# Casts of v moved from ScalarE to POOL in the first block, first normalises brought forward, feed-forward pieces let past waiting hashes

## The chip, the cores and the metric

The kernel runs on one core of one Trainium2 chip. A core has five engines that run side by side, each with its own list of instructions in a fixed order: TensorE (PE in the profile; its weight loads are PEld), VectorE (DVE), ScalarE (ACT), GpSimd (POOL) and SyncE (SP, which here only issues transfers). Sixteen DMA engines move data between the chip's memory and the core. The time is device time in microseconds of the whole program, and less is better.

## The reference

Two steps follow one another. The first is attention with hashed buckets: for each of 4 batches and 8 heads, 768 tokens of 64 features. Six sign bits of a random projection give each query and each key a bucket, and a query attends only to keys of its own bucket.

```
q_bits = (einsum('bhsd,dk->bhsk', q, proj) > 0);  k_bits likewise
q_bucket = sum(q_bits * 2**arange(6));            k_bucket likewise
scores = q @ k.T / 8, -1e9 where the buckets differ
x = softmax(scores) @ v
```

The second is a gated feed-forward layer over the 3072 rows of 512 features that the heads make together:

```
out = x + sigmoid(x @ w_res) * ((gelu(x @ w_gate) * (x @ w_val)) @ w_out)      # 512 -> 1536 -> 512
```

## The kernel before

**Tiling.** The work is cut into eight blocks: 4 batches times two halves of 384 query tokens (`c`). A block has four pairs of heads, and each pair six steps (two heads, three double key tiles), so 24 steps (`LB`). A step `i` is a score product (L579: 128 keys x 384 queries, twice), an exp on ScalarE (L583) and, two steps later in the list, the product with v (`attend`, L607), which TensorE sums into the one av bank in PSUM. After a pair's sixth step VectorE takes the reciprocal of the row sums (L620) and multiplies (L621), which gives `xtok` and frees the av bank for the next pair.

**The hash in the scores.** For each pair, `aug` holds 64 rows of q or k as bf16 and 7 rows made of the hash bits; one product over these 71 rows gives the score and a large penalty where the buckets differ. For the first batch `prep_tokens` fills it: TensorE transposes the tokens (L499), ScalarE and VectorE evacuate them to `trT` (L400), TensorE multiplies by the projection (L462), VectorE makes the bits from PSUM (L426), casts the 64 rows (L418, L416) and moves the bit rows (L436). Part of the second half's rows is cast later. From the second batch on `prep_blocks` does it otherwise: a 32x32 transpose on VectorE (L531), projection (L539), bits (L546), transfers from POOL's queue (L549) and casts (L554).

**v.** `cast_v` (L377) casts a pair's v to bf16 into `vaug`, with a column of ones. Pair 0 and all pairs from the second batch on are cast on POOL, pairs 1 to 3 on ScalarE.

**Feed-forward.** Once a block's four `xtok` are there they are transposed (on TensorE for block 0, L643 and L649; by DMA for later blocks, L629), the gate products run (L661, gelu on ScalarE, L665), and the rest (value L677 and L680, residual L689, output L701, L710, L713, L720) is dealt out in pieces between the attention steps of the next block. Gelu and exp need different tables on ScalarE, so the gelus stand together.

**Loads.** SP loads q, k and v; POOL loads the weights (L361), in the order `wg`, `wv`, `wr`, `wo`, in software-generated transfers that also cast to bf16. The loads of the second batch stand on SP behind a one-element transfer that waits for `wr` (L283).

**What sets the order.** The code first records operations with their engine, an assumed cost, what they read and write, and ring buffers of fixed depth (two score banks, one av bank, three general mm banks, three buffers each for the loaded q, k and v, and so on). `arrange` then plays them out on assumed clocks: on each engine it takes the earliest recorded operation that is ready and whose buffers are free, and emits the instructions in the order of the times it found. A buffer is given only in the order of recording (L186). On the chip each engine runs its list in that order, with semaphore waits. Where TensorE would be idle early on, small products on an idle or unused part of a bank (L830, L833) fill in; their results are not used.

Of the kernel before, what the change touches and what calls it, by code (L numbers as in the profile page):

```python
# [20 lines left out]
def kernel(  # L21
# [54 lines left out]
    made = {name: 0 for name in RINGS}  # L76

    class Buf:


        def __init__(self, ring, make):
            self.ring, self.make, self.tile, self.users, self.taken = ring, make, None, 0, False
            self.place = made[ring]
            made[ring] += 1

# [5 lines left out]
    class Op:  # L91
        __slots__ = ("eng", "cost", "emit", "bufs", "seq", "deps", "left", "users", "ready", "start",
                     "end", "land", "table", "size", "after", "lag", "margin", "opens", "closes", "held", "flight")

    def op(eng, cost, emit, r=(), w=(), table=None, size=0, after=(), lag=0.0, margin=0.0, opens=None, closes=None, held=False, flight=None):
# [8 lines left out]
        o.flight = flight  # L104
        o.seq, o.deps, o.users, o.ready, o.start = len(ops), set(), [], 0.0, None
        o.bufs = []
        for key in (*r, *w):
            b = key[0] if isinstance(key, tuple) else key
            if isinstance(b, Buf) and b not in o.bufs:
                o.bufs.append(b)  # L110
                b.users += 1
        for key in r:
# [23 lines left out]
    def arrange(warm_until, keep_warm):  # L136
# [9 lines left out]
        HOLDS = dict(DVE=("pair", "block"), SP=("xfer",), POOL=("xfer",), ACT=("gelu",))  # L146
        closed = set()
# [6 lines left out]
        def push(o):  # L154
            for e in o.cost:
                heapq.heappush(queue[e], (o.ready, o.seq))
# [6 lines left out]
        while seen < len(ops):  # L163
# [3 lines left out]
            for e in engines:  # L167
                while queue[e] and queue[e][0][0] <= t:
                    heapq.heappush(able[e], heapq.heappop(queue[e])[1])
# [3 lines left out]
                while able[e]:  # L173
                    s = heapq.heappop(able[e])
# [5 lines left out]
                    for b in o.bufs:  # L180
                        line = taken[b.ring]
                        if not b.taken:

                            at = more[b.ring] = more.get(b.ring, len(line) - 1) + 1
                            old = at - RINGS[b.ring]
                            if b.place != at or old >= 0 and gone.get(line[old], 1e9) > t:  # L186
                                fits = False
                    if o.table == "exp" and gelus:
                        fits = False
# [6 lines left out]
                    if fits and e != "PE":  # L196

                        for ready, other in queue[e]:
                            if other < s and ready < t + 0.5 * o.cost[e]:
# [4 lines left out]
                    skipped.append(s)  # L204
                for s in skipped:
                    heapq.heappush(able[e], s)
# [31 lines left out]
                for b in o.bufs:  # L238
# [3 lines left out]
                    b.users -= 1  # L242
                    if b.users == 0:
# [38 lines left out]
    def wait_weights():  # L282
        op("SP", 0.4, lambda: nc.sync.dma_start(mark, wr[0:1, 0, 0:1]), r=["wr"],  # L283
# [72 lines left out]
    mark = const.tile([1, 2], BF16, name="mark")  # L356
# [17 lines left out]
    mark = const.tile([1, 1], BF16, name="mark")  # L374


    def cast_v(n):  # L377
        b, j = pairs[n]
        s = staged[("v", n)]
        cost = VCAST if 0 < n < NPAIR else {"POOL": 0.85}  # L380

# [3 lines left out]
        op(None, cost, emit, r=[(s, 0)], w=[("vaug", b % 2, j)])  # L385

    VCAST = {"ACT": 0.85}
# [485 lines left out]
```

## Time and profile before

| | |
|---|---|
| median of 6 runs | 348.9 us (348.12 to 349.85) |
| the profiled execution's own time | 349.01 us |
| its span | 347.2 us |
| granted TensorE clock | 1.0 |
| exps of L583 | 192, 811 ns each, 149.8 us |
| casts of v | 13 on POOL, 3 on ScalarE (847 ns in the middle) |
| first gate product (L661) | 38.17 us |

The span runs from the first to the last instruction in the profile; the profiled execution took 1.8 us more. Times in the views are microseconds from the span's start. Busy times of matmuls are modelled ends of a pipeline, and the fillers count as busy, so a busy TensorE early in the span need not be a useful one. An engine's idle time is given with what ended it; what a stage costs is read from the stage, not from the average.

### The profile page before, as it was taken

The numbers are of one execution on the slowest core, as the hardware profiler recorded it, in microseconds if no ns is written. First come the engines' busy times: TensorE is split into PE (matmuls) and PEld (weight loads), VectorE is DVE, ScalarE is ACT, GpSimd is POOL, SyncE is SP. The second block draws the span as 40 slices with busy tenths as digits, with TensorE's granted clock in tenths as the row PEclk, the third lists the DMA queues.
The fourth block names the chain that finished last, engine by engine and source line by source line (L and its number), as shares of the span: only waits on it lengthen the run. The fifth ranks groups of instructions, "written<-read, shape, count | busy, mean of one in ns | idle before, by whom it ended". The sixth has DMA issues, their size and how long they took to land.

```text
span 347.2 us, 7664 instructions
## 1 busy us (share of the span) xinstructions
PE 337.0 (97%) x3052; PEld 200.9 (58%) x3076; DVE 190.4 (55%) x344; ACT 236.2 (68%) x341; POOL 61.6 (18%) x101
## 2 busy tenths in 40 slices
PE   8988999999999999999999999999999999999996
PEld 4645666555665566555665556655666556655654
DVE  4997137969689538896363425725052414523353
ACT  3989887755867668665777758675787858775410
POOL 0631000521336310314001220203000100001000
PEclk9999999999999999999999999999999999999999
DMA  7999999999997399987200120021000120012002
GB/s 237 348 215 208 195 159 153 134 174 167 158 149 101 85 192 165 148 92 115 67 13 18 51 71 0 18 55 47 32 14 12 44 72 2 17 49 74 0 2 91
DMA packets 116357, 34.23 MB, mean 99 GB/s; under 512 B 107802, under 2 KB 113698, under 8 KB 116322
## 3 DMA queue, kind: packets, MB, share of 16 engines
q1 hardware_dynamic: 109522, 22.27, 43.8%
q0 software_dynamic: 6496, 11.27, 13.7%
q8 instruction: 24, 0.39, 0.5%
q10 hardware_dynamic: 304, 0.20, 0.2%
q14 instruction: 11, 0.09, 0.1%
HBM read 29.36 MB, written 6.29 MB: 103 GB/s over the span
## 4 chain that ended last, share of the span: by engine, by line
PE 86%; DVE 8%; DMA 3%; ACT 2%; issue 1%; DVEq 0%
PE mm L677 18%; PE mm L661 17%; PE mm L701 16%; PE sc L579 15%; PE av L607 9%; PE mm L689 5%; PE mm L539 3%; DMA xT<-xtok 3%; DVE bits L426 2%; DVE aug L436 2%; ACT e L583 1%; PE idle L830 1%; DVE aug L418 1%; DVE xtok L621 1%; DVE trT L400 1%
## 5 line engine op out<-in xcount | busy, mean ns | idle before, releaser
L583 ACT ACTIVATE e<-sc 128x768 bf16<-128x768 f32 x192 | 149.8, 811 | 50.5 <-PE sc L579 50.1
L680 DVE TENSOR_TENSOR gh<-mm,gh 128x384 bf16<-128x384 f32 x96 | 53.4, 556 | 76.4 <-PE mm L677 62.2
L579 PE MATMUL sc<-aug 71*128 71x384 bf16 x384 | 92.4, 325 | 1.8 <-ACT e L583 1.7
L677 PE MATMUL mm<-xT,wv 128*128 128x384 bf16 x384 | 73.5, 326 | 0.0
L607 PEld LDWEIGHTS <-e 128*128 128x128 bf16 x1152 | 57.0, 97 | 24.0 <-issue 2.5
L701 PE MATMUL mm<-wo,gh 128*128 128x512 bf16 (+2 forms) x303 | 69.0, 362 | 0.4
L661 PE MATMUL mm<-xT,wg 128*128 128x384 bf16 x384 | 66.3, 326 | 1.1 <-DMA xT<-xtok 0.8
L665 ACT ACTIVATE gh<-mm 128x384 bf16<-128x384 f32 x96 | 45.6, 492 | 31.6 <-PE mm L661 31.3
L607 PE MATMUL av<-vaug,e 128*128 128x65 bf16 x1152 | 62.2, 193 | 1.4 <-DVE xtok L621 1.4
L661 PEld LDWEIGHTS <-wg 128*128 128x128 bf16 x384 | 37.0, 98 | 26.2 <-issue 1.8
L579 PEld LDWEIGHTS <-aug 71*128 71x128 bf16 x384 | 34.8, 98 | 29.2 <-issue 5.4
L677 PEld LDWEIGHTS <-wv 128*128 128x128 bf16 x384 | 34.0, 98 | 21.5 <-issue 3.1
L701 PEld LDWEIGHTS <-gh 128*128 128x128 bf16 x312 | 27.2, 98 | 26.0 <-issue 1.9
L710 DVE SCALAR_TENSOR_TENSOR y<-th,mm 128x512 f32<-128x512 bf16 x23 | 15.8, 687 | 45.7 <-PE mm L701 40.6
L549 POOL DMA_DIRECT2D aug<-bits x48 | 27.9, 585 | 68.7 <-DVE bits L546 68.3
L720 POOL DMA_DIRECT2D out_dram<-o x21 | 13.0, 620 | 134.0 <-DVE rec L620 106.3
L692 ACT ACTIVATE th<-mm 128x512 bf16<-128x512 f32 x24 | 14.4, 598 | 16.5 <-PE mm L689 16.5
L554 DVE TENSOR_SCALAR aug<-trT 64x1536 bf16<-64x1536 f32 x24 | 23.5, 979 | 1.1 <-PE sc L579 0.4
L689 PE MATMUL mm<-wr,xT 128*128 128x512 bf16 x81 | 22.9, 379 | 0.8
L384 POOL CAST vaug<-vs 128x768 bf16<-128x768 f32 x13 | 11.4, 874 | 46.8 <-DMA vs<-in_v_dram 32.5
L546 DVE TENSOR_SCALAR bits<-mm,shift 128x384 bf16<-128x384 f32 x24 | 13.6, 609 | 10.7 <-PE mm L539 10.5
L621 DVE TENSOR_TENSOR xtok<-av,rec 128x384 bf16<-128x384 f32 x32 | 17.8, 558 | 1.1
(58 smaller groups left out, 168.5 us busy)
## 6 DMA issues: line engine op xcount, KB each, us to landing
vs<-in_v_dram SPq DMA_DIRECT2D x16, 384.0 KB
out_dram<-o POOLq DMA_DIRECT2D x21, 256.0 KB, 2.5
qs<-in_q_dram SPq DMA_DIRECT2D x48, 96.0 KB
ks<-in_k_dram SPq DMA_DIRECT2D x48, 96.0 KB
wg<-in_moe_w_gate_dram POOLq DMA_DIRECT2D x4, 384.0 KB, 9.8
wv<-in_moe_w_val_dram POOLq DMA_DIRECT2D x4, 384.0 KB, 15.2
wo<-in_moe_w_out_dram POOLq DMA_DIRECT2D x4, 384.0 KB, 15.7
qs<-in_q_dram SPq DMA_DIRECT2D x3, 384.0 KB
```

What stands on the lines that cost most here:

```text
L549: op("POOL", 0.6, lambda i=i: nc.gpsimd.dma_start(a[D:KAUG, :, i * CH:(i + 1) * CH], bits()[32 * i:32 * i + NR]), r=[(bits, 0), (bits, 1)] ...
L554: lambda hh=hh: nc.vector.tensor_scalar_mul(a[0:D, hh, :], trT()[hh * D:(hh + 1) * D].rearrange("d s n -> d (s n)"), QKS),
L579: nc.tensor.matmul(sp()[:, x, 0:CH], a[:, S + jt * P:S + (jt + 1) * P], a[:, c * CH:(c + 1) * CH], start=True, stop=True)
L583: op("ACT", 0.72, lambda: nc.scalar.activation(e(), sp()[:, :, 0:CH], AF.Exp, scale=EXPS), r=[sp], w=[e], table="exp", held=True, opens=(" ...
L607: nc.tensor.matmul(av()[:, o:o + D + 1], e()[:, x, t * P:(t + 1) * P], va[:, 2 * j + hh, TS[b][jt], :], start=(first and x == 0 and t == 0 ...
L621: op("DVE", 0.48, lambda: nc.vector.tensor_mul(xt()[:, j].rearrange("p t (h d) -> p h t d", h=2), view()[:, :, :, 0:D], rec().to_broadcast ...
L661: nc.tensor.matmul(ps()[:, 0:CH], wg[:, kk, m * P:(m + 1) * P], x()[:, kk, :], start=(kk == 0), stop=(kk == KM - 1))
L665: op("ACT", 0.385, lambda: nc.scalar.activation(g()[:, m, :], ps()[:, 0:CH], AF.Gelu), r=[ps], w=[(g, m)], table="gelu", closes=("gelu", u ...
L677: nc.tensor.matmul(ps()[:, 0:CH], wv[:, kk, m * P:(m + 1) * P], x()[:, kk, :], start=(kk == 0), stop=(kk == KM - 1))
L680: op("DVE", 0.46, lambda m=m, ps=ps: nc.vector.tensor_mul(g()[:, m, :], ps()[:, 0:CH], g()[:, m, :]), r=[ps], w=[(g, m)])
L689: nc.tensor.matmul(rps(), x()[:, kk, t * P:(t + 1) * P], wr[:, kk, :], start=(kk == 0), stop=(kk == KM - 1))
L701: nc.tensor.matmul(ps()[:, 0:W], g()[:, kk, t * P:(t + 1) * P], wo[:, kk, cols], start=(kk == 0), stop=(kk == KF - 1))
```

## The change

- `cast_v`: in the first block the casts of pairs 1 to 3 move from ScalarE to POOL. Each is preceded on POOL by a copy of one element of the pair's `aug` tile into `mark`, recorded as reading the pair's late key-side cast (and the one before it), so the cast cannot start before VectorE has finished them and turned to the hash bits.
- The two normalise operations of block 0 (`u == 0`) get `urgent=URG`, which puts them ahead of operations recorded up to 200 earlier on VectorE. The first av product of each pair of that block gets a margin of 0.4 us in the plan.
- The feed-forward products of value, residual and output get `over=True`: they may take an mm bank ahead of an earlier recorded operation, if that one isn't ready yet. Before, banks went strictly in order of recording.
- Some assumed costs change: evacuation, bits, reciprocal, product. They change only the order.
- `mark` is one tile of two elements; L283 writes the first.

The functions are the same ones; the order on all engines is played out anew.

```diff
     class Buf:
         def __init__(self, ring, make):
...
+            if self.place == 0:
+                lines[ring] = []
+            lines[ring].append(self)
...
-        o.flight = flight
+        o.flight, o.over = flight, over
+        o.key = len(ops) - urgent
...
+                b.taker = b.taker or o
...
                     for b in o.bufs:
                         line = taken[b.ring]
                         if not b.taken:
                             at = more[b.ring] = more.get(b.ring, len(line) - 1) + 1
                             old = at - RINGS[b.ring]
-                            if b.place != at or old >= 0 and gone.get(line[old], 1e9) > t:
+                            if old >= 0 and gone.get(line[old], 1e9) > t:
                                 fits = False
+                            for c in lines[b.ring][first.get(b.ring, 0):b.place]:
+                                if not c.taken and c.taker is not o and (not o.over or c.taker.left == 0 and c.taker.ready <= t):
+                                    fits = False
+                                    break
...
     def cast_v(n):
         b, j = pairs[n]
         s = staged[("v", n)]
+        r = [(s, 0)]
+        if 0 < n < NPAIR:
+            a = aug_of(n)
+            op("POOL", 0.1, lambda: nc.gpsimd.tensor_copy(mark[:, 1:2], a[0:1, 1, S + CH:S + CH + 1]),
+               r=[("aug", n % NAUG, 1, 1, 1, "d"), ("aug", n % NAUG, 1, 1, 0, "d")], w=["turn"])
+            r.append("turn")
         cost = VCAST if 0 < n < NPAIR else {"POOL": 0.85}
...
-        op(None, cost, emit, r=[(s, 0)], w=[("vaug", b % 2, j)])
-
-    VCAST = {"ACT": 0.85}
+        op(None, cost, emit, r=r, w=[("vaug", b % 2, j)])
+
+    VCAST = {"POOL": 0.85}
...
-            cost = {"DVE": 0.09 + width * 0.00107, "ACT": 0.12 + width * 0.00088}
+            cost = {"DVE": (0.25 if width > CH else 0.12) + width * 0.00107, "ACT": 0.08 + width * 0.00088}
...
+    URG, AVM = 200, 0.4
...
-        op("PE", 0.18, emit, r=[e, ("vaug", b % 2, j)], w=[av])
+        op("PE", 0.18, emit, r=[e, ("vaug", b % 2, j)], w=[av], margin=AVM if first and u == 0 else 0.0)
...
-            op("DVE", 0.21, lambda: nc.vector.reciprocal(rec(), view()[:, :, :, D:D + 1]), r=[av], w=[rec])
-            op("DVE", 0.48, lambda: nc.vector.tensor_mul(
+            op("DVE", 0.23, lambda: nc.vector.reciprocal(rec(), view()[:, :, :, D:D + 1]), r=[av], w=[rec], urgent=URG if u == 0 else 0)
+            op("DVE", 0.56, lambda: nc.vector.tensor_mul(
...
-               closes=("pair", i // PS))
+               closes=("pair", i // PS), urgent=URG if u == 0 else 0)
...
-            op("PE", 0.65, emit, r=[(x, kk) for kk in range(KM)] + [("wv", kk) for kk in range(KM)], w=[ps])
+            op("PE", 0.65, emit, r=[(x, kk) for kk in range(KM)] + [("wv", kk) for kk in range(KM)], w=[ps], over=True)
...
-            op("PE", 0.87, emit, r=[(x, kk) for kk in range(KM)] + ["wr"], w=[rps])
+            op("PE", 0.87, emit, r=[(x, kk) for kk in range(KM)] + ["wr"], w=[rps], over=True)
...
-                       w=[ps])
+                       w=[ps], over=True)
```

## The prediction

> **What bounds the kernel now.** First the page's shares of busy time.
>
> ```profile
> PE 337.0 (97%) x3052; PEld 200.9 (58%) x3076; DVE 190.4 (55%) x344; ACT 236.2 (68%) x341; POOL 61.6 (18%) x101
> ```
>
> TensorE is busy almost throughout, but an average over stages hides where it isn't. So next the busy time by stretches of the span (after the stretch: its length, then busy time and instruction count of each engine, clock, DMA share, GB/s).
>
> ```profile
> 15.00:20.00 5.00, 5.00 (x71) 3.70 (x71) 4.71 (x10) 4.92 (x8) 1.76 (x3) 1.00 1.10 236
> 20.00:25.00 5.00, 3.49 (x44) 2.20 (x49) 4.74 (x11) 3.63 (x7) 1.55 (x3) 1.00 1.09 215
> 25.00:30.00 5.00, 4.07 (x64) 2.27 (x49) 4.79 (x12) 4.98 (x7) 1.59 (x2) 1.00 1.07 211
> 30.00:35.00 5.00, 4.62 (x74) 3.50 (x73) 2.42 (x6) 4.58 (x7) 0.00 (x0) 1.00 1.21 206
> ...
> 40.00:45.00 5.00, 5.00 (x32) 3.03 (x31) 0.00 (x0) 3.95 (x9) 0.00 (x0) 1.00 1.18 165
> ...
> 120.00:140.00 20.00, 20.00 (x177) 12.24 (x176) 12.17 (x19) 14.12 (x23) 3.43 (x5) 1.00 1.29 172
> ```
>
> From 40 us to 330 us TensorE lacks only about 2.3 us in all (my sum over the stretches): there the time is matmuls, and the change takes none away. From 10 to 38 us it is otherwise: ScalarE and VectorE are both near full, and TensorE's 5.00 contain the fillers of L833, which do nothing. Until the first block's attention is done the feed-forward (FF) cannot start (first L661 matmul at 38.17). So the question is what ends at 38.17. ScalarE in order of time (start, duration, instruction, idle before it):
>
> ```profile
> 14.58 0.85 ACT L384 CAST vaug<-vs 128x768 bf16<-128x768 f32 x1
> 15.51 0.60 ACT L400 ACTIVATE trT<-mm 128x512 f32<-128x512 f32 x1
> ...
> 19.32 0.85 ACT L384 CAST vaug<-vs 128x768 bf16<-128x768 f32 x1
> ...
> 24.84 0.81 ACT L583 ACTIVATE e<-sc 128x768 bf16<-128x768 f32 x1 [0.60 <-PE sc L579]
> 25.55 0.83 ACT L384 CAST vaug<-vs 128x768 bf16<-128x768 f32 x1
> 26.27 3.71 ACT L583 ACTIVATE e<-sc 128x768 bf16<-128x768 f32 x5
> 30.38 6.04 ACT L583 ACTIVATE e<-sc 128x768 bf16<-128x768 f32 x8 [0.41 <-PE sc L579]
> ```
>
> Three v casts stand between the exps. I count the exps from 0: exp 8 starts at 20.66, 11 at 24.84, 17 at 30.38, and exp 23, the block's last, at 34.86 (30.38 + 6 steps of 0.747). Twice the row idles for a score. The same two moments on TensorE:
>
> ```profile
> 23.71 0.71 PE L607 MATMUL av<-vaug,e 128*128 128x65 bf16 x18 [1.19 <-DVE xtok L621]
> ...
> 29.25 0.71 PE L607 MATMUL av<-vaug,e 128*128 128x65 bf16 x18 [0.18 <-DVE xtok L621]
> ```
>
> The next pair's first av matmul needs the one av bank, so it stands still until VectorE has normalised the pair before. And VectorE comes to that late:
>
> ```profile
> 21.60 1.25 DVE L436 COPY aug<-bits 7x384 bf16<-7x384 bf16 x4
> 22.87 0.20 DVE L620 RECIPROCAL rec<-av 128x6 f32<-128x6 f32 x1
> 23.10 0.56 DVE L621 TENSOR_TENSOR xtok<-av,rec 128x384 bf16<-128x384 f32 x1
> ```
>
> Pair 0's last av matmuls ended at 18.7, its normalise ran at 22.87: it sat behind pair 2's whole preparation. Both waits and the casts are what the change touches.
>
> **The change, part by part.** The order of instructions in the two built programs says what moves. *Casts:* three leave ScalarE for POOL; each follows a one-element copy that reads pair n's last aug cast (L416). *Normalise:* pair 0's goes ahead of pair 2's aug casts, pair 1's ahead of pair 3's hash bits. *TensorE:* the first avs follow their exps singly instead of 18 at a time, and hashes stand a little later. *Weights:* on POOL's queue three wg loads now stand behind cast 1, four wv behind cast 2, wr and wo behind cast 3. *Blocks 1 and 2:* some hashes and FF pieces change places; from block 3 on the order is almost as it was.
>
> Row steps used: score to its exp 0.58 (24.25 to 24.84); exp to exp 0.70, and 0.73 to 0.75 where two score banks alternate; exp start until its score bank is free again 0.87 (26.27 to 27.14); token transposes (L499) to ScalarE's evacuation 0.69 (19.47 to 20.16), which takes 0.50; av to reciprocal 0.39 (36.07 to 36.46); product (L621) to next av 0.61 (23.10 to 23.71); a hash (L462) 0.8; pair preparation on VectorE as its row: 0.95, 0.56, bits 1.14, moves 1.29, evacuation 0.69.
>
> Walk. Up to exp 5 (16.7) nothing is gained: without the cast at 14.58 the evacuation still waits for transposes at 14.81, so it runs at 15.5 as before. Cast 1's 0.85 is worth nothing. Exps 6 and 7 run at 18.0 and 18.7; exp 8 no longer waits for a cast and an evacuation, 19.45. Pair 0's last av is at 18.1, VectorE frees from its evacuation at 18.62: reciprocal 18.65, product 18.88, first av of pair 1 at 19.49. The hash of pair 2 stands behind that av: 19.67 to 20.5 (18.66 before, a loss of 1.0 there), transposes 20.5, evacuation 21.17, exp 9 at 21.67 (22.73 before), exp 10 at 22.37. VectorE: 19.47 casts, bits 21.03 to 22.2, which free the banks for the last transposes at 22.33; evacuation 23.02, exp 11 at 23.57 (before 24.84: 1.27 gained). Pair 3's hash needs VectorE's evacuation, which follows pair 2's moves (22.2 to 23.45) and ends at 24.2; with the score ahead of it, it runs 24.8 to 25.6, and pair 1's last av stands behind it, 25.6. So a new wait: exp 14 at 26.38 with ScalarE idle 0.6. Reciprocal 26.0, product 26.22, next av 26.83; exp 17 at 28.68 (before 30.38). Pair 3's bits 26.81 to 27.95, moves to 29.23 (28.38 before, since two normalises of 0.76 now precede them); their first head is there at 28.78, exp 18 at 29.38, exp 23 at 33.2 by bank-paced steps of 0.73 to 0.75 (34.86 before). Front gain 1.7 us. The same by ScalarE's account: casts 2 and 3 leave (0.84 and 0.72 by the next start) and three idles of before (0.77 at 22.23, 0.60, 0.41), 3.3 in all; new idles come, 1.0 before the evacuation at 21.17, 0.6 at exp 14, 0.15 at exp 17, so 1.6 stay.
>
> Behind exp 23 stand the same instructions as before: av, normalise, transposes, copy, gates. FF would start at 38.17 - 1.7 = 36.5, and the 309 us behind it are matmuls that shift as a whole.
>
> *Weights on POOL.* Before, wg was issued from 11.2, wv from 13.4, wr at 19.3; now about 16.6, 22.1 and 27. Covered by the DMA stream: one weight tile lands about every 2 us (wo's four issues waited for wg tiles until 21.0, 23.4, 25.3; the first wg took 7.8 us from issue). From 16.6 the last wg lands near 25 to 27 and is needed at 36.5; wv before landed by 32.5, needed at 44.5; wr before at 35.0. wr also opens SP's queue: the one-element DMA on SP (L283) waited 6.4 us for it, and behind it stand the loads of pair 4 (v landed at 49.87, q is transposed at 56 or later). Price nothing while the stream is less than about 7 us late.
>
> *Casts on POOL.* Median 0.839 in the row, from 0.822 to 1.337. The spread is the point here:
>
> ```profile
> 80.55 0.84 POOL L384 CAST vaug<-vs 128x768 bf16<-128x768 f32 x1
> 80.60 2.58 DVE L554 TENSOR_SCALAR aug<-trT 64x1536 bf16<-64x1536 f32 x2
> ...
> 85.08 1.92 DVE L554 TENSOR_SCALAR aug<-trT 64x1536 bf16<-64x1536 f32 x2
> ```
>
> Where a POOL cast started just ahead of two VectorE ops on SBUF they took 0.66 longer. The Trainium skill, page "SBUF — State Buffer", section "Who interferes with whom", speaks against this change: the port pair that VectorE and GpSimd share is an exclusive lock, and the loser is held up for the whole instruction; a VectorE op with at most one SBUF input, outside the modes that use two ports, stays clear of it. By the rule alone, casts beside the aug casts would cost 3 x about 0.8 = 2.4 us on a full VectorE and end at 349.6, slower than before; by the row it is 0.66 each, 2.0, and 349.2. Neither applies if the cast lies beside L426: bits on PSUM took 0.62 beside the cast at 10.42, 0.61 without. Cast 1 starts about 0.3 after L416's end at 15.40 (the copy 0.1, the hand-over 0.2: an estimate) and ends at 16.53; bits end at 16.57. It just fits; a slip costs itself. Then the wg and wv issues lie beside the moves, of which one took 0.496 for 0.250 beside a cast and one 0.35 beside an issue, while the last four took 1.29 beside an issue and 1.29 alone. Bounds for eight moves 0 to 0.8; I take 0.2, nearer the group that lay beside an issue unharmed.
>
> *Reorder of blocks 1 and 2.* Bound from both sides: it can win back part of the 2.3 us that TensorE lacks after 40 us (about 1.0 of it lies in these blocks, up to 120 us), or make matmuls wait for one of three mm banks, 0.3 at each of four or five moved hashes (my estimate from VectorE's 0.69 for y against the score and av work of about 0.5 between). Taken as 0.
>
> Sum: 347.2 - 1.7 + 0.2 = 345.7 of span. The profiled execution took 349.01, 1.8 around its span: 347.5. The median of the runs is 0.1 lower: 347.4.
>
> **Rivals.** *The gain is spent downstream:* hashes that were overtaken hold mm banks later, and the residual matmuls (L689) wait for y: 4 x 0.3 = 1.2 given back, 348.6. For it: three mm banks; against: the hash waits on TensorE in those blocks are 0.3 at most now. *Slower, by the shared ports:* in 15.4 to 29.2 VectorE has no gap, so every blocked instruction delays exp 18. Three casts at 0.66 and seven issues at 0.25 make 3.7, minus the front's 1.7 gives 350.9. It decides from 1.7 us of added VectorE time, and is slower beyond measurement from 2.4. Against it: the placement beside PSUM reads, and the moves at 27.09 unharmed by an issue. *Weights late:* needs a shift of over 7 us; I see 1 to 3, so it stays at the forecast's 347.4. *More than forecast:* nothing lost on the ports (0.2), no idle at exp 14 (0.6), half of the 1.0 won by the reorder (0.5): 346.1. *It does not do what it says:* the hold fails to place the casts; that is the ports rival in part.
>
> **Numbers.** Forecast (gain of 1.0 to 2.1; own range 346.8 to 347.9) 0.62; more 0.09; spent downstream 0.15, of which a quarter still over 0.2% faster; ports 0.10; slower by something unnamed in the reordered blocks 0.04. A measurement can tell 0.2%, 0.7 us, from no change. Faster 0.62 + 0.09 + 0.04 = 0.75, same 0.11, slower 0.14. The range takes in the spent case and leaves out the ports and the largest gains: 346.4 to 349.1.
>
> **What would show it.** Right: POOL's first-block casts of 0.82 to 0.9 within the bits; ScalarE's exp 11 near 23.6, exp 17 near 28.7; no wait of av for xtok over 0.3; first L661 near 36.5; TensorE as full as before behind it. Wrong: L416, L418 or L436 longer than their rows, a gate matmul waiting for a weight load, VectorE's aug of pair 3 later than 29.5, or L689 and L701 waiting for VectorE in 60 to 120 us.

## The result, and the profile after

The changed kernel takes 348.02 us (median of 32 runs, 345.34 to 351.69) against 348.77 us of the kernel before (69 runs, 346.64 to 352.21). The ratio is 0.9976, with a 95% interval of 0.9963 to 0.9989. So it is a little faster, by 0.24%, and 348.02 lies in the predicted range (346.4 to 349.1), 0.6 us above the predicted 347.4. The profiled execution of the changed kernel took 347.02 us, 1.0 less than its own median, with a span of 345.2 us; the prediction's sum for the span was 345.7. Medians are over all executions; a ratio leaves out those that took over 1.5% longer than the fastest of their kernel, so a median can lie above that of before while the ratio is 1.

Line numbers moved: L283 is now L296, L361 L373, L384 (cast of v) L403, L400 L419, L416 L435, L418 L437, L426 L445, L436 L455, L462 L481, L499 L518, L579 L599, L583 L603, L607 L627, L620 L640, L621 L641, L629 L649, L661 L681, L677 L697, L689 L709, L701 L721. The one-element copy is L396.

ScalarE in order of time (start, duration, instruction, idle before it and what ended it). These rows answer to those shown of before:

```profile
17.59 2.26 ACT L603 ACTIVATE e<-sc 128x768 bf16<-128x768 f32 x3
20.95 0.60 ACT L419 ACTIVATE trT<-mm 128x512 f32<-128x512 f32 x1 [1.10 <-PE mm L518]
...
23.37 2.34 ACT L603 ACTIVATE e<-sc 128x768 bf16<-128x768 f32 x3
26.32 9.14 ACT L603 ACTIVATE e<-sc 128x768 bf16<-128x768 f32 x12 [0.61 <-PE sc L599]
```

The casts are gone from this list, and idles have come in their place: 0.61 before the evacuation at 15.15, 1.10 before that at 20.95 and 0.61 before exp 14. Exp 11 starts at 23.37 (24.84 before), and from 26.32 the exps run without a break at 0.76 each, which puts exp 23 at about 33.1 (34.86 before). VectorE:

```profile
18.25 0.18 DVE L640 RECIPROCAL rec<-av 128x6 f32<-128x6 f32 x1
18.47 0.56 DVE L641 TENSOR_TENSOR xtok<-av,rec 128x384 bf16<-128x384 f32 x1
...
21.66 1.44 DVE L455 COPY aug<-bits 7x384 bf16<-7x384 bf16 x4
...
26.16 0.56 DVE L641 TENSOR_TENSOR xtok<-av,rec 128x384 bf16<-128x384 f32 x1
```

Pair 0 is normalised at 18.25 instead of 22.87. Four moves of bit rows took 1.44 here (1.25 before). POOL, with the copy that holds the cast and the cast itself:

```profile
15.09 0.18 POOL L396 COPY mark<-aug 1x1 bf16<-1x1 bf16 x1 [3.49 <-DVE aug L435]
15.21 0.82 POOL L403 CAST vaug<-vs 128x768 bf16<-128x768 f32 x1
```

TensorE's waits in the first block, and then the passage from block 1 to block 2, where block 1's gate products need its transposed `xtok` (`xT`) from SP's queue, pair by pair; the row of before for the same place stands last:

```profile
19.18 0.34 PE L627 MATMUL av<-vaug,e 128*128 128x65 bf16 x6 [0.24 <-DVE xtok L641]
...
26.87 0.52 PE L627 MATMUL av<-vaug,e 128*128 128x65 bf16 x12 [0.32 <-DVE xtok L641]
...
78.16 1.79 PE L681 MATMUL mm<-xT,wg 128*128 128x384 bf16 x10 [1.06 <-DMA xT<-xtok]
```
```profile
80.54 0.65 PE L661 MATMUL mm<-xT,wg 128*128 128x384 bf16 x3 [0.59 <-DMA xT<-xtok]
```

The waits for `xtok` are 0.24 and 0.32 (1.19 and 0.18 before), and the first gate product of block 0 starts at 36.17 (38.17 before). But at 78.16 TensorE waits 1.06 us for a transfer, where before it waited 0.59. By the stretches, between 70 and 80 us it is busy 8.88 of 10 us, where it had been busy 9.84 (before, then after):

```profile
70.00:80.00 10.00, 9.84 (x69) 5.24 (x70) 6.83 (x12) 4.90 (x6) 2.85 (x6) 1.00 1.04 167
70.00:80.00 10.00, 8.88 (x73) 4.97 (x72) 7.75 (x12) 5.86 (x8) 4.23 (x7) 1.00 0.95 175
```

The wait of before lies on both sides of the 80 us mark, so this pair of rows overstates the loss. From the first gate product to the end both traces need 309.0 us: what the front gains is not lost in this trace, but nothing is won behind it either. The chain that ended last, by engine:

```profile
PE 88%; DVE 4%; DMA 3%; ACT 3%; issue 1%; POOL 0%; ACTq 0%; POOLq 0%; DVEq 0%
```

Before, this row began with PE 86% and DVE 8%. VectorE has lost half of its share, and ScalarE is still on the chain with 3% (before 2%), though its casts are gone.

### The profile page after: what moved, and what is told of

It is laid out like the page before. It is cut to its first block, busy times and chain, and to the rows that moved or that the text cites. A ratio compares the mean times of both kernels' runs of the same rounds, so it can differ in the third digit from the quotient of the medians.

```text
span 345.2 us, 7696 instructions
## 1 busy us (share of the span) xinstructions
PE 336.1 (97%) x3064; PEld 200.4 (58%) x3088; DVE 192.0 (56%) x344; ACT 234.4 (68%) x338; POOL 62.0 (18%) x107
## 4 chain that ended last, share of the span: by engine, by line
PE 88%; DVE 4%; DMA 3%; ACT 3%; issue 1%; POOL 0%; ACTq 0%; POOLq 0%; DVEq 0%
PE mm L697 18%; PE mm L681 18%; PE mm L721 16%; PE sc L599 16%; PE av L627 9%; PE mm L709 6%; PE mm L558 3%; ACT e L603 2%; DMA xT<-xtok 2%; DMA proj_pair<-in_proj_dram 1%; DVE bits L445 1%; DVE aug L455 1%; PE mm L481 0%; PE mm L518 0%; DVE trT L419 0%
## 5 line engine op out<-in xcount | busy, mean ns | idle before, releaser
L603 ACT ACTIVATE e<-sc 128x768 bf16<-128x768 f32 x192 | 150.1, 811 | 52.2 <-PE sc L599 51.8
L599 PE MATMUL sc<-aug 71*128 71x384 bf16 x384 | 92.3, 325 | 1.1 <-ACT e L603 0.9
L697 PE MATMUL mm<-xT,wv 128*128 128x384 bf16 x384 | 73.3, 326 | 0.0
L627 PEld LDWEIGHTS <-e 128*128 128x128 bf16 x1152 | 57.1, 97 | 24.3 <-issue 1.8
L721 PE MATMUL mm<-wo,gh 128*128 128x512 bf16 (+2 forms) x303 | 69.0, 362 | 0.4
L681 PE MATMUL mm<-xT,wg 128*128 128x384 bf16 x384 | 66.2, 326 | 1.3 <-DMA xT<-xtok 1.1
L627 PE MATMUL av<-vaug,e 128*128 128x65 bf16 x1152 | 62.7, 193 | 0.6 <-DVE xtok L641 0.6
L681 PEld LDWEIGHTS <-wg 128*128 128x128 bf16 x384 | 36.9, 98 | 26.2 <-issue 2.0
L599 PEld LDWEIGHTS <-aug 71*128 71x128 bf16 x384 | 34.8, 98 | 28.6 <-issue 4.6
L697 PEld LDWEIGHTS <-wv 128*128 128x128 bf16 x384 | 34.0, 98 | 21.5 <-issue 3.1
L721 PEld LDWEIGHTS <-gh 128*128 128x128 bf16 x312 | 27.2, 98 | 24.6 <-issue 0.6
L568 POOL DMA_DIRECT2D aug<-bits x48 | 26.9, 564 | 66.6 <-DVE bits L565 65.9
L573 DVE TENSOR_SCALAR aug<-trT 64x1536 bf16<-64x1536 f32 x24 | 24.4, 1016 | 1.1 <-PE sc L599 0.4
L709 PE MATMUL mm<-wr,xT 128*128 128x512 bf16 x81 | 22.9, 379 | 0.8
L403 POOL CAST vaug<-vs 128x768 bf16<-128x768 f32 x16 | 13.3, 833 | 47.3 <-DMA vs<-in_v_dram 38.5
L641 DVE TENSOR_TENSOR xtok<-av,rec 128x384 bf16<-128x384 f32 x32 | 17.8, 557 | 1.1
```

What stands on the lines that cost most here:

```text
L568: op("POOL", 0.6, lambda i=i: nc.gpsimd.dma_start(a[D:KAUG, :, i * CH:(i + 1) * CH], bits()[32 * i:32 * i + NR]), r=[(bits, 0), (bits, 1)] ...
L573: lambda hh=hh: nc.vector.tensor_scalar_mul(a[0:D, hh, :], trT()[hh * D:(hh + 1) * D].rearrange("d s n -> d (s n)"), QKS),
L599: nc.tensor.matmul(sp()[:, x, 0:CH], a[:, S + jt * P:S + (jt + 1) * P], a[:, c * CH:(c + 1) * CH], start=True, stop=True)
L603: op("ACT", 0.72, lambda: nc.scalar.activation(e(), sp()[:, :, 0:CH], AF.Exp, scale=EXPS), r=[sp], w=[e], table="exp", held=True, opens=(" ...
L627: nc.tensor.matmul(av()[:, o:o + D + 1], e()[:, x, t * P:(t + 1) * P], va[:, 2 * j + hh, TS[b][jt], :], start=(first and x == 0 and t == 0 ...
L641: op("DVE", 0.56, lambda: nc.vector.tensor_mul(xt()[:, j].rearrange("p t (h d) -> p h t d", h=2), view()[:, :, :, 0:D], rec().to_broadcast ...
```

## The experiments

The first exp of an execution starts anywhere from 9.1 to 10.8 us after the start of the span, in all these traces, so absolute times of two traces are not comparable within 1 us. The table therefore counts from the first exp to the first gate product ("front"), and from there to the end of the span ("behind"). The last column is TensorE's waiting for `xT` at the passage from block 1 to 2. Front, behind and wait are those of one execution each, while the median is over all of them.

| kernel | casts of pairs 1 to 3 | normalise early | FF overtakes | median us | ratio to before, 95% | front | behind | wait for xT |
|---|---|---|---|---|---|---|---|---|
| before, two traces | ScalarE | no | no | 348.6 to 348.8 | 1 | 27.57, 27.23 | 309.0, 309.3 | 0.59, 1.29 |
| changed | POOL, held | yes | yes | 348.02 | 0.9976 (0.9963 to 0.9989) | 25.81 | 309.0 | 1.06 |
| again | POOL, held | yes | yes | 347.07 | 0.9947 (0.9928 to 0.9966) | 26.18 | 309.9 | 1.94 |
| no_hold | POOL, at once | yes | yes | 347.76 | 0.9978 (0.9958 to 0.9997) | 27.11 | 308.5 | 0.62 |
| no_over | POOL, held | yes | no | 347.13 | 0.9961 (0.9948 to 0.9973) | 25.69 | 308.8 | 0 |
| no_over_b | POOL, held | yes | no | 346.77 | 0.9937 (0.9909 to 0.9965) | 25.67 | 308.6 | 0 |
| casts_only | POOL, held | no | no | 349.60 | 1.0022 (1.0009 to 1.0036) | 26.46 | 311.0 | 2.00 |
| norm_only | ScalarE | yes | no | 346.39 | 0.9937 (0.9914 to 0.9961) | 26.46 | 308.2 | 0 |
| norm_b | ScalarE | yes | no | 346.38 | 0.9929 (0.9908 to 0.9949) | 26.38 | 308.3 | 0 |
| norm_over | ScalarE | yes | yes | 346.31 | 0.9928 (0.9906 to 0.9950) | 26.60 | 308.2 | 0 |
| late_mark | ScalarE | yes | no | 346.74 | 0.9958 (0.9934 to 0.9983) | 26.00 | 308.4 | 0 |
| gate_wv | POOL, held | yes | yes | 349.12 | 1.0000 (0.9978 to 1.0023) | 25.71 | 308.4 | 0.58 |
| late_xT | POOL, held | yes | yes | 351.50 | 1.0065 (1.0043 to 1.0087) | 26.15 | 314.0 | 3.56 |

The rows casts_only and norm_only do not isolate a part completely. The changed assumed costs stay in both, so each differs from before by its part and by these costs, and "normalise early" stands for the urgency together with the margin of 0.4 us. Exactly one part changes from norm_b to no_over_b (the casts), from norm_b to norm_over and from no_over to again (the overtaking), and from casts_only to no_over (the normalise with its margin, 349.60 to 347.13, each against a kernel before of 348.6 to 348.8).

**again.** The changed kernel, unaltered, measured a second time.

> The changed kernel unaltered, for a second look and for the spread. Known so far: its profiled span is 345.2 us against 347.2 us before, its median 0.24% below before, so the profile shows a gain of 2.0 us and the median one of 0.8. Theory A (front gain constant, later loss): the first gate matmul lies at 36.0 to 36.6 us in any execution, and what differs between executions comes behind it, in waits of TensorE for the transposed x or for the second batch's loads between 60 and 120 us. Theory B (front gain itself varies): in a slower execution the first gate matmul lies at 37.2 us or later. Theory C (clock): executions at a granted clock below 1.0 are about 1 to 2 us longer, and the changed kernel has more of them than the one before. Ratio expected 0.996 to 0.999 by all three.

347.07 us, ratio 0.9947. The front is 26.18 (25.81), and the wait for `xT` 1.94 (1.06), so theory A's reading stands; the size of the gain is 0.24% and 0.53% in the two measurements (0.7 and 1.7 us). Theory C is half right. Executions with a mean granted clock below 0.998 are longer, by 3.5 us at the median (1 to 2 expected), but the changed kernel has fewer of them, not more: 4 of 22, against 48 of 65 of the kernel before. Between the executions at 0.998 or more the gain is 1.0 us (346.9 against 347.9), so a part of the 1.7 is the clock.

**no_hold.** The copies that hold the casts are left out; the rest of the lists on TensorE, VectorE and ScalarE is the same.

```diff
-        if 0 < n < NPAIR:
+        if False:
```

> The changed kernel without the one-element copies on POOL: TensorE, VectorE and ScalarE keep the same lists, the casts stand where their loads land and the weights are issued early as before. By the prediction's sum the hold keeps casts beside PSUM reads: without it casts 1 to 3 lie beside L436, L437 and L435, each costs VectorE up to 0.66 us, together 0.7 to 2.0 us at the first gate matmul (37 to 38 us), ratio to before 0.999 to 1.001. Rival (weights late is the loss): issuing the weights early again opens SP's queue near 35.0 instead of 36.1 and wins more than the ports cost, ratio 0.994 to 0.996.

The front is 27.11, 0.9 longer than in again, and the median is 0.7 us above again on the same chip; the two intervals just overlap. The ratio, 0.9978, lies between the two forecasts. SP's opening did not come earlier (36.01), so the rival was not put to the test. Two casts on POOL now fall beside VectorE's aug casts. VectorE, then POOL, of no_hold:

```profile
12.78 1.44 DVE L437 CAST aug<-trT 64x1536 bf16<-64x1536 f32 x1
14.23 1.37 DVE L435 CAST aug<-trT 64x768 bf16<-64x768 f32 x1
```
```profile
12.57 0.83 POOL L403 CAST vaug<-vs 128x768 bf16<-128x768 f32 x1 [2.33 <-DMA vs<-in_v_dram]
14.33 0.84 POOL L403 CAST vaug<-vs 128x768 bf16<-128x768 f32 x1
```

Held, the same two took 0.95 and 0.56 in again. So 0.49 and 0.81 were added; the POOL cast at 14.33 lasts 0.84, and L435 lost practically all of it. The hold does what it is for. Of the two prices that the prediction weighed, 0.66 from the row and 0.8 from the rule of exclusive ports, the second was met by L435; L437, which began when 0.62 us of the first POOL cast were left, lost less than either. The third cast, at 18.14, lay beside an evacuation from PSUM (L419), which took 0.69 as always.

**no_over.** Feed-forward pieces wait in line for banks as before.

```diff
-            op("PE", 0.65, emit, r=[...], w=[ps], over=True)
+            op("PE", 0.65, emit, r=[...], w=[ps])
```
(and likewise for the residual and output products)

> The changed kernel with banks again given in the order of recording (over off): the front keeps its gain, only blocks 1 and 2 are ordered otherwise. The prediction took this edit as 0: ratio equal to the changed kernel within 0.0015. Rival (gain spent downstream by overtaken hashes): 0.002 to 0.0035 faster than the changed kernel, with shorter waits of TensorE between 60 and 80 us.

347.13 us, the same as again (347.07) on the same chip, as the prediction took it; the front is 25.69. Block 1's gate products now run through, in one row with no wait:

```profile
77.04 2.37 PE L681 MATMUL mm<-xT,wg 128*128 128x384 bf16 x12
```

So letting the pieces past brings no measurable time. With the casts on POOL the wait for `xT` goes with it, but it is not enough for that wait, as norm_over shows below; and a trace without the wait belongs here to the same median as a trace with 1.94 of it.

**gate_wv.** SP's loads of the second batch are opened by the last `wv` instead of by `wr`, which the change made later on POOL's queue. The plan is played out anew with this, and other lists move too: at the passage to block 2 six gate products now stand ahead of a score, where in again two scores and two av groups come first.

```diff
-        op("SP", 0.4, lambda: nc.sync.dma_start(mark[:, 0:1], wr[0:1, 0, 0:1]), r=["wr"],
+        op("SP", 0.4, lambda: nc.sync.dma_start(mark[:, 0:1], wv[0:1, 3, 0:1]), r=[("wv", 3)],
```

> The changed kernel with the second batch's loads opened by the last wv instead of wr (SP's one-element transfer reads wv). Theory A with the loads as its cause: SP's loads start about 2 to 3 us earlier, the waits for the transposed x at 76 to 80 us shrink, ratio 0.001 to 0.003 below the changed kernel. If the loads aren't what is late: within 0.001 of it, or slower, since loads and wr, wo then share the DMA engines.

The transfer on SP stood at 33.00 instead of 35.32 (again), but nothing came of it: the first pair's loads of q and k then took 6.01 and 5.73 us on SP, beside the transfers of `wr` and `wo`, where they had taken 6.21 and 2.75 in again. So the third transpose was issued at 70.73, hardly earlier than in again (70.98). The wait for `xT` fell to 0.58 (for the fourth transpose; the third was in time), and yet the ratio is 1.0000, no gain. The profiled execution itself was quick (346.23), but 12 of the 22 executions had a clock below 0.998, and these took 350.6 at the median against 347.6 for the others. The opening is not what the loads wait for; that they wait for the transfers' throughput fits the longer k loads and is not tested by itself.

**casts_only.** The casts on POOL with their hold, and no early normalise, no overtaking.

```diff
-    URG, AVM = 200, 0.4
+    URG, AVM = 0, 0.0
```
(and `over=True` off as in no_over)

> The casts alone: POOL with the hold, but normalises in their old rank, no margin, banks in the order of recording. TensorE keeps its 1.2 us stall for pair 0's normalise. Front: exps 8 and 12 to 16 come earlier, exp 11 still waits; first gate matmul 37.2 to 37.8 us, ratio 0.997 to 0.999. On the clock: the kernel before ran at a granted clock of about 0.994 in 48 of 65 executions, and the changed one without overtaking in 0 of 20. If the stall in the front is what lowers the clock, at least half the executions here are low; if it is something else that this kernel lost, few are.

349.60 us, ratio 1.0022, where 0.997 to 0.999 was expected: without the early normalise, the casts on POOL (with the changed costs) make the kernel no faster and a little slower. The front is 0.8 to 1.1 shorter than before, but the normalise is still late. VectorE of casts_only:

```profile
20.28 0.18 DVE L640 RECIPROCAL rec<-av 128x6 f32<-128x6 f32 x1
...
23.02 0.56 DVE L641 TENSOR_TENSOR xtok<-av,rec 128x384 bf16<-128x384 f32 x1
```

The product of pair 0 waits behind bits and moves until 23.02 (23.10 before). And what the front gains is lost at the passage to block 2, where TensorE waits twice (the second time 1.58, in all 2.00):

```profile
78.38 0.81 PE L681 MATMUL mm<-xT,wg 128*128 128x384 bf16 x4 [0.42 <-DMA xT<-xtok]
80.77 1.14 PE L681 MATMUL mm<-xT,wg 128*128 128x384 bf16 x6 [1.58 <-DMA xT<-xtok]
```

On the clock, 15 of 20 executions were below 0.998, as expected if a stall in the front lowers it; but the stall that was to stay is only 0.34 in this trace (1.19 before).

**norm_only, and norm_b.** The early normalise alone: casts of pairs 1 to 3 on ScalarE as before, no copies, no overtaking. The changed costs and the margin are kept. norm_b is the same kernel on another chip.

```diff
-    VCAST = {"POOL": 0.85}
+    VCAST = {"ACT": 0.85}
...
-        if 0 < n < NPAIR:
+        if False:
```
(and `over=True` off)

> The early normalises alone: casts of v stay on ScalarE, no hold, banks in the order of recording. Both av stalls go, ScalarE keeps its 2.5 us of casts: first gate matmul 36.9 to 37.8 us, ratio 0.997 to 0.999. On the clock: if the stall of 1.2 us in the front lowers it, few executions here are low (under a quarter).

> The kernel of norm_only once more, on another chip: casts of pairs 1 to 3 on ScalarE, normalises of the first block early, no feed-forward piece let past a hash. If the early normalise is the whole gain, the ratio to the kernel before is again 0.992 to 0.996. If the first measurement, of 7 executions, was luck, it is 0.996 to 1.000.

346.39 and 346.38 us, ratios 0.9937 and 0.9929: the best kernel of the study, faster than before by 0.6 to 0.7% and faster than the full change, with one part of it alone. norm_only was expected at 0.997 to 0.999: more was won than foretold, 1.1 and 0.8 in the front and about as much again behind it (308.2 against 309.0 and 309.3). None of the 17 executions was below 0.998. ScalarE and TensorE of norm_b:

```profile
24.34 0.86 ACT L403 CAST vaug<-vs 128x768 bf16<-128x768 f32 x1
25.07 10.57 ACT L603 ACTIVATE e<-sc 128x768 bf16<-128x768 f32 x14
```
```profile
75.55 1.14 PE L681 MATMUL mm<-xT,wg 128*128 128x384 bf16 x6
...
76.85 1.42 PE L681 MATMUL mm<-xT,wg 128*128 128x384 bf16 x6
```

With the third cast still on ScalarE, exps 13 to 26 follow it without an idle: the cast lies just ahead of exp 13, where in the changed kernel ScalarE waits 0.61 for a score ahead of exp 14. And behind the front block 1's gate products find their `xT`.

**norm_over and no_over_b**, on the chip of norm_b: one adds the overtaking to it, the other puts its casts on POOL with the hold.

> As norm_b, with the feed-forward pieces let past waiting hashes. If letting them past is what brings on the wait for xT between blocks 1 and 2 (TensorE done with the block before xT's transfer lands), that wait shows here by 0.5 to 1.5 us, and the time is 0.5 to 1.5 us above norm_b. If it is worth nothing, as the prediction took it, both are equal within 0.3 us, and no wait shows.

> As norm_b, with the casts of pairs 1 to 3 on POOL behind the one-element copies. By the prediction's account of ScalarE the casts that leave are worth 0.84 and 0.72 less the new idles, so this would be some 0.5 to 1 us faster than norm_b. If the casts on ScalarE lie in time in which it would wait anyway, both are equal within 0.4 us, and the first gate product stands at the same distance from the first exp within 0.5 us.

346.31 and 346.77 us against 346.38. The overtaking changes nothing in the time, and no wait for `xT` comes with it; my theory that overtaking brings on that wait falls in this form. The casts on POOL shorten the front by 0.7 (25.67 against 26.38), but the time is not shorter: 346.77, 0.1% above norm_b, less than the intervals can separate. (The two traces need 334.3 and 334.7 from the first exp to the end, which is no clear difference either.) Of the two expectations, ScalarE's account (0.5 to 1 us faster) is not met by the median, and that both fronts would agree within 0.5 us is not met either: a shorter front without a measurably shorter time.

**late_xT.** The changed kernel with two one-element transfers on SP ahead of block 1's last transpose.

```diff
-                op("SP", 1.25, lambda: nc.sync.dma_start_transpose(...),
+                def xfer():
+                    for _ in range(2 if u == 1 and j == NPAIR - 1 else 0):
+                        nc.sync.dma_start(mark[:, 0:1], wr[0:1, 0, 0:1])
+                    nc.sync.dma_start_transpose(...)
+                op("SP", 1.25, xfer,
```

> The changed kernel with two one-element transfers on SP ahead of the last transpose of block 1; the second waits until the first has landed, so the transpose comes 3 to 5 us later; all other lists are the same. If the wait for the transposed x at about 77 us is what lowers the clock in some executions of the changed kernel (4 of 22 and 8 of 33 so far, each about 3 us longer), then most executions here are at 0.995 or less, the lowered stretch stands behind that wait, and the time rises by the longer wait plus 1.5 to 2 us: ratio 1.006 to 1.016 to the kernel before. Rival: the clock has nothing to do with that wait; then the low executions stay at about a fifth and the time rises by the longer wait alone, ratio 1.002 to 1.008.

351.50 us, and 18 of 20 executions were below 0.998, as the theory had it; the ratio, 1.0065, lies in both forecasts. The time is 4.4 above again, each against a kernel before of 348.6 to 348.8. TensorE waits twice for `xT`, 3.56 in all (1.94 in again), which is 1.6 more:

```profile
78.51 1.80 PE L685 MATMUL mm<-xT,wg 128*128 128x384 bf16 x7 [2.31 <-DMA xT<-xtok]
81.56 1.12 PE L685 MATMUL mm<-xT,wg 128*128 128x384 bf16 x3 [1.25 <-DMA xT<-xtok]
```

The first wait is for the third transpose, which the edit leaves alone (SP reached it at 73.40, 2.4 later than in again, for no reason that the edit gives); only the second is for the fourth, which the edit put at 79.19. The rest shows in the stretches (columns as in the prediction):

```profile
75.00:80.00 5.00, 2.69 (x25) 1.58 (x23) 4.89 (x6) 2.09 (x2) 1.68 (x3) 0.92 0.54 138
80.00:85.00 5.00, 3.75 (x17) 1.80 (x16) 3.52 (x4) 1.29 (x4) 0.00 (x0) 0.50 0.78 128
85.00:90.00 5.00, 5.00 (x29) 2.90 (x28) 0.00 (x0) 3.40 (x7) 0.00 (x0) 0.90 1.47 170
...
79.00:80.00 1.00, 1.00 (x5) 0.53 (x4) 0.97 (x2) 0.00 (x0) 0.00 (x0) 0.58 0.00 0
```

By stretches of 1 us (the last row is one of them) the clock is 1.00 up to 79, 0.58 from 79 to 80, 0.50 up to 86 and 1.00 from there on. So it fell near 79.2, after the first wait and before the second, and stayed at half for some 6.8 us. An estimate from these rows: TensorE worked through 5.6 of them (6.8 less the second wait) at half rate, which costs 2.8, and with 1.6 of waiting that makes the 4.4. The added waiting alone is the smaller part of the price.

**before_again.** The kernel before once more, for a second trace.

> The kernel before once more, for a trace. In three of four executions it runs at a granted clock of about 0.994. If this one does, the lowered stretch is expected in the front, between 20 and 32 us, behind the stalls for pair 0's normalise and for the scores; then it costs less than in dense matmuls (low executions of before are about 1.1 us longer than the others, low ones of the changed kernel about 3 us).

347.91 us, span 346.1. Its first gate product is 27.23 after the first exp (27.57 in the other trace), the two waits for `xtok` are 1.25 and 0.29, and the wait for `xT` at block 1 to 2 is 1.29. So the kernel before has that wait too; it isn't made by the change. This execution ran at a granted clock of 1.00, so where the lowered stretch of the kernel before lies was not seen.

**late_mark.** norm_b, with the transfer that opens SP's loads reading from `wo`'s first tile, so that it stands later; every other list is the same.

```diff
-        op("SP", 0.4, lambda: nc.sync.dma_start(mark[:, 0:1], wr[0:1, 0, 0:1]), r=["wr"],
+        op("SP", 0.4, lambda: nc.sync.dma_start(mark[:, 0:1], wo[0:1, 0, 0:1]), r=["wr"],
```

> The kernel of norm_b with one element changed: the transfer on SP that opens the loads of the second batch reads from wo's first tile instead of wr, so it waits about 2 us longer (the first wo is issued 2.1 us after wr in norm_b and takes as long to land). Every list of instructions is otherwise the same. Theory: SP's queue is a chain from that transfer to xT of block 1 (35.3 to 36.6 us in all runs), so what opens it 2 us later puts xT 2 us later against TensorE. Then the transfer stands near 36.4, the first gate product stays at 26.4 after the first exp, TensorE waits for xT 0.5 to 2.5 us at the passage from block 1 to 2, the time is 0.5 to 2 us above norm_b (346.4), and where that wait brings on the lowered clock, some 3 us more in a good part of the executions, none of which showed it in norm_b. Rival: the loads have slack (the prediction's view: price nothing while the weights are less than about 7 us late), the chain takes up the 2 us, no wait appears, the time is that of norm_b within 0.4 us, and the clock stays full.

SP's opening, and TensorE at the passage:

```profile
37.59 0.63 SPq L296 DMA_DIRECT2D mark<-wo  x1
```
```profile
76.68 1.14 PE L681 MATMUL mm<-xT,wg 128*128 128x384 bf16 x6
```

It opened at 37.59, which is 26.84 after the first exp (25.03 in norm_b), 1.8 later, and no wait for `xT` appeared: 346.74 us against 346.38, in overlapping intervals. The theory that SP's queue is a rigid chain from the opening to `xT` fell. The chain took up the delay: from the opening to block 1's third transpose it was 33.2 us here and 36.0 in norm_b. The rival, the prediction's own view that the weights may be some us late, held, by 1.8 us and in this kernel.

## Why the prediction was right or wrong

**The walk of the front was right, nearly line by line.** The trace of after starts its first exp 0.24 earlier than that of before, and the steps lie earlier by about as much: the reciprocal at 18.25 (18.65 foretold), product 18.47 (18.88), first av of pair 1 at 19.18 (19.49), its hash at 19.45 (19.67), evacuation 20.95 (21.17), exp 9 at 21.44 (21.67), exp 11 at 23.37 (23.57). Cast 1 was worth nothing: the evacuation behind it waits for transposes (0.61, L518) where the cast had been. The "new wait" before exp 14 came as said, 26.32 and 0.61 idle against 26.38 and 0.6, as did the 1.0 before the evacuation (1.10). Pair 1's product ran at 26.16 (26.22), the next av at 26.87 (26.83). The front gained 1.76 from the first exp in the traces compared (25.81 against 27.57), and by 1.05 in the least favourable pair of the four (26.18 against 27.23); 1.7 was foretold.

**The ports step was right, its term a little small.** With the hold, L437 and L435 kept 0.95 and 0.56. The moves beside POOL's issues and casts were the term estimated at 0.2: the three groups of four took 1.38, 1.44 and 1.36 against 1.29 in the prediction's row, 0.3 in all. The rival by ports did not come, and no_hold shows what it would have cost here: 0.9 of front and 0.7 us in the median, a gain made smaller, not a loss.

**The weights step was right.** The opening on SP stood at 36.10 (34.99 before), and no gate product waited for a weight. late_mark shows such slack in norm_b.

**The weakest step was "the 309 us behind it are matmuls that shift as a whole",** and with it "reorder of blocks 1 and 2: taken as 0". Behind the first gate product the two traces of the kernel before need 309.0 and 309.3, the changed kernel 309.0 and 309.9, and the kernels with the early normalise alone 308.2 to 308.4. In the first trace the step held, so the sum came out (345.2 of span for 345.7, of which 0.24 is only the earlier first exp); over the kernels this stretch was worth from -1 to +0.7 us, on a sum of -1.5. The bound of about 1.0 to win was the right one, and norm_only, norm_b and norm_over reach it. In the changed kernel's traces TensorE waits 1.06 and 1.94 for `xT` at the passage from block 1 to block 2 instead. I had looked only at the other transfers of SP, the loads of pair 4, and not at the transposes of `xtok` that stand behind pair 7's loads on the same queue. The view that would have said so was on record: the wait of 0.59 at 80.54 in the trace of before was in the 2.3 us that I counted as there to be won, and FF that starts 1.7 earlier can make such a wait longer as well. That this wait is what keeps the changed kernel from the time of norm_b is argued, not shown: no_over has no such wait in its trace and still needs 308.8, gate_wv waits 0.58 and needs 308.4, and no_over and again have the same median.

What the traces say of the wait: SP issues the third transpose of block 1 between 70.3 and 72.8 in all of them but late_xT, and TensorE comes to block 1's first gate product 39.4 to 41.2 after block 0's. In the changed kernel, again, no_hold and casts_only it stops there for the third transpose, which it can use 6.7, 7.4, 6.4 and 5.6 after the issue. In gate_wv it runs past the third within 5.2 of its issue, in norm_b and norm_only within 5.6 and 6.1. So it is not TensorE's lead alone that decides: the time from issue to use differs by over 2 us. In the two traces of the kernel before and in gate_wv TensorE waits only for the fourth. Why the third transpose takes longer in some kernels is not settled: neither the opening (late_mark, gate_wv) nor the overtaking (norm_over) is enough by itself, and with one trace or two for each kernel it may also differ between executions of one kernel.

**The median also holds the clock, which the sum left out.** 8 of 33 executions of the changed kernel and 4 of 22 in again were below 0.998, and about 3 us longer; of the kernel before 48 of 65 were, beside again, and 1.1 us longer. The median of the changed kernel moved by nearly 1 us between its two measurements, 348.02 and 347.07, to both sides of the forecast's 347.4; that a sum of such terms comes within some tenths is luck.

**"The same by ScalarE's account" hid which part brings the gain.** It let casts 2 and 3 leave with 1.56, added the old idles (1.78) and took off 1.75 of new idles, as one sum. norm_b shows the parts: with all three casts still on ScalarE the three old idles are gone, with one new of 0.83 at 16.28, so they belong to the late normalise. Taking the casts off as well (no_over_b) puts idles of 0.61, 0.96 and 0.61 where they had been, and of 2.5 us of casts 0.7 stays in the front (26.38 to 25.67). In the whole time nothing measurable stays of that (346.77 against 346.38), and casts_only is slower than before (1.0022), while the kernels with the early normalise alone have the full gain (0.9937 and 0.9929). The front alone would mislead here: casts_only shortens it by 0.8 to 1.1, as much as norm_only does (both 26.46), and loses it again behind. The sign of the forecast rested on the right mechanism, VectorE's lateness, but had the casts been made alone, the account of ScalarE would have forecast a gain where there is a small loss.

**The rivals.** "The gain is spent downstream" was in part right as to fact (309.9 behind the front in again, 309.0 in the first trace) and wrong as to place: no residual or output product (L709, L721) waited for VectorE; the gates waited for a transfer. The measured 348.02 lies between that rival's 348.6 and the forecast's 347.4, and again's 347.07 lies on the forecast's side.

## What to carry to other kernels

Follow a gain at the front to the next place where the engine that gained meets something of another pace, such as a transfer behind a queue of loads, and compare when the engine gets there with when the transfer lands; here the transfer's own time from issue to use, 5.2 us at most in one kernel and 7.4 in another, moved as much as the gain. Of a change with several parts, test each alone: the part that took most busy time from a full engine's list (three casts, 2.5 us) was worth nothing measurable, and the one that only moved normalises of 0.76 us each forward in their queue (with a margin in the plan) was worth 2.2 us. An idle that an engine must have anyway is a free place for work, so see whether work taken off it leaves the idle behind.

## What the hardware showed that I had not expected

**The clock after a wait.** In late_xT a wait of 2.31 us, up to 78.51, was followed from about 79.2 by 6.8 us at a granted clock of 0.50; TensorE was busy 2.69 of the 5 us from 75 to 80. The Trainium skill, page "TensorE: Matmul & The Clock Gate", section "Part 1: The HAM clock gate (the "warmup" mystery)", says that TensorE goes to half rate after an idle window of about 3.4 us. The half rate agrees; no wait here was that long, and by this trace a shorter one between thin work is enough. It isn't always: the trace of again has a wait of 1.94 at the same place and stays at 1.00.

How often an execution has a mean clock below 0.998 goes with the kernel. It was 2 of 66 in the six measurements whose trace shows no wait for `xT` (no_over, no_over_b, norm_only, norm_b, norm_over, late_mark). With a wait it was 8 of 33 in the changed kernel, 4 of 22 in again, 4 of 14 in no_hold, 12 of 22 in gate_wv, 15 of 20 in casts_only and 18 of 20 in late_xT; in the kernel before 48 of 65 beside again, 24 of 42 beside late_xT and 15 of 37 beside norm_b and late_mark. That is a correlation: all profiled executions but that of late_xT ran at 0.999 or 1.00, and in late_xT the clock fell before the wait that the edit made. It may also have more than one origin. In the kernels with the early normalise the low executions are 2.4 to 4.0 us longer than the others where there are several of both; in casts_only and the kernel before, where the normalise is late, only 0.7 to 1.1. A fall in the front, where TensorE is less full, would fit that, and no trace here has caught it.

**A cast on POOL beside one on VectorE** cost VectorE almost its whole length: in no_hold L435 took 1.37 for 0.56 beside a POOL cast of 0.84. Beside VectorE work that reads PSUM nothing was added: with the hold, the bits (L445) took 1.13 to 1.14 beside the same casts, 1.14 before. The order of magnitude was in the trace of before (0.66); how near to the whole it can come was not.
